# A decayed linear attention followed by two matrix products: four stages share a 512-column first product, and the whole program is written as one list

## The chip, the cores and the metric

The kernel runs on one core of a Trainium2 chip. A core has TensorE (PE, with its weight loads shown as PEld), VectorE (DVE), ScalarE (ACT), GpSimd (POOL) and SyncE (SP). Each engine executes its own instructions in the order in which the program lists them, and waits on semaphores for what other engines produce. The metric is the device time of one execution in microseconds (us), the median of several runs; lower is better.

## The reference

The first part is a recurrence over 768 tokens, for 4 batches and 8 heads of width 48. The second part is a two-layer product over all 3072 tokens.

```python
for t in range(S):
    cur = einsum('bhd,bhe->bhde', u * kt, vt)
    y[:, :, t] = einsum('bhd,bhde->bhe', rt, state + cur)
    state = w[:, :, None] * state + einsum('bhd,bhe->bhde', kt, vt)
x = y.transpose(0, 2, 1, 3).reshape(3072, 384)
h = x @ w_in                      # 384 -> 2048
out = maximum(0.01 * h, h) @ w_out   # 2048 -> 384
```

## The kernel before, in words

The tokens are cut into 24 stages of 128 tokens. Stage n is batch n mod 4 and block n div 4 of that batch, so the state that stage n produces is needed by stage n + 4. Operands are bf16, sums are float32. PSUM has 8 banks of 128 x 512 float32; a bank is taken by a product and given back when another engine has read it out, in the order of the list. Each operation of a stage has a letter, which the list ORDER uses with the stage's number:

- `r`, `k`, `v`: load of the stage's r, k, v block, issued on POOL (line 220; stage 0's r and k go over SP and ACT, line 211). `wi`, `wo`: a quarter of w_in, w_out, issued on POOL (lines 230, 234).
- `Pq`, `Pk`: r and k times a decay table, on DVE (line 361), into `qk`. `X..T`: transposing DMA of `qk` into `tp`, issued on SP (line 366), from stage 6 on. Stages 0 to 5 are transposed on PE instead (`T`, line 424) and copied out by ACT or DVE (`t`).
- `A`: the 128 x 128 score products of 8 heads on PE (line 453), into two banks. `Ma`, `Mb`: on DVE, the strictly causal part of each bank is written into `at` (line 466; line 462 for stages 0 to 3).
- `q`: the diagonal u term, three instructions on DVE (lines 390, 392, 394: `ku`, `rku`, and their sum per head `s_tok`). `Q`: two instructions on POOL (line 401) that write the diagonal matrices into `at`, ahead of `M`. For stages 0 to 3 the diagonal goes another way (`X`, `D`, and `Q` on DVE).
- `Y`: y of the stage, transposed, on PE (line 592): 12 products from the state and 16 from `at`, in strips of 32 columns. `y`: ACT copies it to `xT` (line 606).
- `K`: k-transposed times v on PE (line 494). `S`: the new state on DVE (lines 557, or 560 and 562).
- `G`, `J`: first product with w_in on PE, for one stage (128 columns, line 631) or a pair (256 columns, line 654); `g`, `j`: ACT applies the leaky relu and writes `gT` (lines 641, 664). `H`: second product with w_out on PE, 16 matmuls of 384 columns (line 678); `h`: ACT copies it out (line 690) and SP stores it (line 692).
- `F`: n matmuls on a tile of ones whose result is not used (line 267). `E`, `TQ`, `TK`, `Cw`, `Cu`, `C`, `W`, `U` and their like prepare tables.

The program is written by ORDER up to the first products of the pair 2 (stages 4 and 5) and the loads of stage 11. Then a loop takes pair m = 3 to 11: 8 first products `J` with their `j`; among or behind them `A` of the next pair; `P`, `X` of the pair after it, `M`, the loads three pairs ahead (held back until a product of the pair has been done), `q` and `Q`; `H` of the pair m - 1, with `Y`, `K`, `S` of the next pair between its two halves. The last `H` is split in two so that its store is short. `Sched.add` notes for each operation what it reads and writes, and `resolve` turns these into semaphore waits: one engine's order is the list's order, and a wait at the head of an engine holds everything behind it.

Of the kernel before, what the change touches and what calls it, by code (L numbers as in the profile page):

```python
# [30 lines left out]
T3q U t5q@ r4 t3q G2.1 Q1 utab A3 wi0 X3 g2.1 G0.3 M1b wo0 M3b D3 K3 g0.3 Y1 v5 M3a G2.3 y1 Q3 k6 G1.3 P4k g2.3 q5 k7
Y3 g1.3 T4k y3 v4 G1.1 t4k S3 G3.2 wo1 g1.1 P4q P5k G3.1 Q5 g3.2 S1 T5k g3.1 T4q G3.3 q4 t4q G0.0 t5k r6 g3.3 A4 A5
g0.0 P0k G3.0 Q4 M5a K0 G1.2 g3.0 M5b S0 K5 G2.2 g1.2 wo3 G2.0 M4a g2.2 wo2 P7k G1.0 g2.0 P6k M4b r7 K4 Y5 g1.0 S4 Y4
r9 y5 G0.2 S5 y4 k9 J2.7 g0.2 q6 r8 J2.5 j2.7 J2.6 k8 j2.5 J2.4 P6q j2.6 Q6 J2.0 X6T j2.4 J2.1 j2.0 J2.2 j2.1 k10 H2
j2.2 P7q q7 v6 X7T v7 P9q v8 H3 P9k h2 q9 X9T Q7 P8q H1 h3 Q9 q8 v9 P8k A6 h1 X8T A7 M6b H0 Q8 M6a M7b M7a v11 K7 Y6 h0
# [91 lines left out]
def bass_rwkv5_eagle__then__act_leaky_relu_kernel(  # L127
# [494 lines left out]
    def g1(n, grp):  # L622
        ps_g, key = g_bank[n, grp] = take()
        m, half = divmod(n, 2)
        ix, t = m % NX, slice(128 * half, 128 * half + 128)

        def emit():
            for f in range(4):
                fb = 4 * grp + f
                for s in range(NSL):  # L630
                    last = PE.matmul(ps_g[:, 128 * f:128 * f + 128], w_in_sb[:, s, 128 * fb:128 * fb + 128],  # L631
                                     xT[ix][:, s, t], start=s == 0, stop=s == NSL - 1)
# [12 lines left out]

    def g1_pair(m, j):
        ps_g, key = g_bank[m, j, 2] = take()
        ix = m % NX

        def emit():  # L650
            for f in range(2):
                fb = 2 * j + f
                for s in range(NSL):
# [176 lines left out]
```

## Time and profile before

| | |
|---|---|
| runs, median (lowest to highest) | 169.99 us (169.92 to 170.53), 3 runs |
| profiled execution | 170.09 us, span of its trace 168.3 us |
| granted TensorE clock, mean | 0.999 |
| PE busy | 161.6 us, 96% of the span |
| DVE, ACT, POOL busy | 110.2, 91.0, 111.1 us |
| data moved by DMA | 20.18 MB, mean 120 GB/s |

The profile gives, for each engine, groups of instructions with their busy time and the mean duration of one, the idle time ahead of them with what ended it, and the chain of work that ended last. A matmul's duration includes its way through the array and overlaps the next one's, so a product's cost is read from the distance between starts, not from its mean. A line of the timeline is: start, length, engine, line of the kernel, operation, output and inputs, shape, count, and in brackets the idle time before it and what ended that.

### The profile page before, as it was taken

What the parts mean: (1) busy time and instruction counts of PE and PEld (TensorE: products, weight loads), DVE (VectorE), ACT (ScalarE), POOL (GpSimd) and SP (SyncE); (2) the same over time, 40 slices, a digit from 0 to 9 for tenths busy, and PEclk for the clock granted to TensorE, in tenths of its full rate; (3) what the DMA queues carried; (4) which work ended last, traced back from release to release, by engine and by line L of the source; (5) the groups of instructions that cost most, each with busy time, mean ns of one, the idle gap of its engine ahead of it and who ended that gap; (6) DMA issues with size and microseconds to landing.
All of it is one profiled execution on the core that took longest, in us unless ns stands there. A gap on an engine that the chain in (4) does not pass through costs nothing.

```text
span 168.3 us, 4915 instructions
## 1 busy us (share of the span) xinstructions
PE 161.6 (96%) x2116; PEld 122.6 (73%) x2116; DVE 110.2 (66%) x221; ACT 91.0 (54%) x168; POOL 111.1 (66%) x125
## 2 busy tenths in 40 slices
PE   5889979999999999999999999999999999999994
PEld 5767869986568768768668768768678678668663
DVE  7499978828992497497599998996996805000000
ACT  4658777892228537537436536537537447449221
POOL 7999996999699929939939976975960540000000
PEclk9999999999999999999999999999999999999999
DMA  7999999999999996995994995994999111011012
GB/s 108 105 157 162 171 192 167 150 170 155 150 230 150 118 95 186 80 126 156 90 147 129 125 162 142 153 97 113 146 104 143 32 47 51 0 51 47 29 65 95
DMA packets 101263, 20.18 MB, mean 120 GB/s; under 512 B 94457, under 2 KB 101242, under 8 KB 101242
## 3 DMA queue, kind: packets, MB, share of 16 engines
q0 software_dynamic: 76512, 10.03, 93.3%
q1 hardware_dynamic: 23690, 9.64, 28.1%
q8 instruction: 16, 0.26, 0.7%
q10 hardware_dynamic: 1040, 0.20, 0.6%
q14 instruction: 5, 0.04, 0.1%
HBM read 20.45 MB, written 4.72 MB: 150 GB/s over the span
## 4 chain that ended last, share of the span: by engine, by line
PE 69%; POOL 12%; DMA 9%; DVE 7%; issue 1%; ACT 0%; POOLq 0%; DVEq 0%
PE ps L678 31%; PE ps L654 29%; DMA k_sb<-in_k_dram 5%; PE ps L592 5%; DMA r_sb<-in_r_dram 4%; POOL r_sb L220 3%; DVE qk L361 3%; PE ps L453 3%; POOL k_sb L220 3%; POOL v_sb L220 2%; PE ps L494 2%; DVE at L466 1%; POOL at L401 1%; POOL w_in_sb L230 1%; DVE rku L392 1%; DVE ku L390 1%
## 5 line engine op out<-in xcount | busy, mean ns | idle before, releaser
L678 PE MATMUL ps<-w_out_sb,gT 128*128 128x384 bf16 (+2 forms) x400 | 65.6, 320 | 0.0
L401 POOL TENSOR_TENSOR at<-ident,s_tok 128x512 bf16<-128x512 bf16 x40 | 42.8, 1101 | 21.0 <-DVE s_tok L394 21.0
L654 PE MATMUL ps<-xT,w_in_sb 128*128 128x256 bf16 x480 | 54.9, 273 | 0.0
L678 PEld LDWEIGHTS ps<-w_out_sb,gT 128*128 128x128 bf16 x400 | 37.7, 98 | 22.4
L664 ACT ACTIVATE gT<-ps 128x512 bf16<-128x512 f32 x80 | 47.8, 597 | 8.7 <-PE ps L654 4.0
L654 PEld LDWEIGHTS ps<-xT,w_in_sb 128*128 128x128 bf16 x480 | 46.4, 98 | 6.7
L690 ACT ACTIVATE out_sb<-ps 128x384 f32<-128x384 f32 (+2 forms) x25 | 12.0, 479 | 55.8 <-PE ps L678 55.8
L466 DVE CAST_PREDICATED at<-mask,ps 128x512 bf16<-128x512 uint16 x40 | 25.0, 684 | 21.8 <-PE ps L453 21.8
L220 POOL DMA_DIRECT2D k_sb<-in_k_dram x23 | 21.1, 923 | 3.3 <-PE ps L654 3.3
L220 POOL DMA_DIRECT2D v_sb<-in_v_dram x24 | 22.2, 925 | 0.8 <-POOLq L815 0.8
L220 POOL DMA_DIRECT2D r_sb<-in_r_dram x23 | 21.0, 914 | 0.0
L392 DVE TENSOR_TENSOR rku<-r_sb,ku 128x384 bf16<-128x384 bf16 x20 | 17.8, 892 | 0.7
L631 PE MATMUL ps<-xT,w_in_sb 128*128 128x128 bf16 x192 | 12.6, 219 | 0.5 <-DMA w_in_sb<-in_moe_w_in_dram 0.5
L606 ACT ACTIVATE xT<-ps 128x384 bf16<-128x384 f32 x24 | 10.9, 491 | 2.3 <-PE ps L592 2.2
L361 DVE TENSOR_TENSOR qk<-r_sb,qtab 128x384 bf16<-128x384 bf16 x23 | 9.1, 400 | 4.5 <-DMA r_sb<-in_r_dram 4.1
L631 PEld LDWEIGHTS ps<-xT,w_in_sb 128*128 128x128 bf16 x192 | 10.9, 98 | 1.3 <-DMA w_in_sb<-in_moe_w_in_dram 0.7
L394 DVE TENSOR_REDUCE s_tok<-rku 128x8 f32<-128x384 bf16 x20 | 11.1, 553 | 0.7
L641 ACT ACTIVATE gT<-ps 128x512 bf16<-128x512 f32 x16 | 9.5, 599 | 3.4 <-PE ps L631 2.9
L562 DVE TENSOR_TENSOR st<-sum_t,wl 128x384 bf16<-128x384 bf16 x16 | 10.7, 672 | 0.5
L592 PE MATMUL ps<-at,v_sb 128*32 128x128 bf16 x384 | 10.7, 219 | 0.0
L361 DVE TENSOR_TENSOR qk<-k_sb,ktab 128x384 bf16<-128x384 bf16 x23 | 9.9, 434 | 0.7 <-DMA k_sb<-in_k_dram 0.7
L592 PEld LDWEIGHTS ps<-tp,st 128*32 128x32 bf16 x240 | 7.2, 96 | 3.1 <-issue 2.5
(64 smaller groups left out, 120.9 us busy)
## 6 DMA issues: line engine op xcount, KB each, us to landing
out_dram<-out_sb SPq DMA_DIRECT2D x23, 192.0 KB, 2.2
v_sb<-in_v_dram POOLq DMA_DIRECT2D x24, 96.0 KB, 5.3
r_sb<-in_r_dram POOLq DMA_DIRECT2D x23, 96.0 KB, 5.4
k_sb<-in_k_dram POOLq DMA_DIRECT2D x23, 96.0 KB, 5.1
w_in_sb<-in_moe_w_in_dram POOLq DMA_DIRECT2D x4, 384.0 KB, 7.0
w_out_sb<-in_moe_w_out_dram POOLq DMA_DIRECT2D x4, 384.0 KB, 8.5
tp<-qk SPq DMA_TRANSPOSE x18, 4.1
k_f<-in_k_dram ACTq DMA_DIRECT2D x1, 192.0 KB, 2.8
```

The source lines that it names most:

```text
L220: add("pool", lambda: G.dma_start(dst, src), R=pace, W=[(which, n)], dma=f"{which}{n}")
L361: add("dve", lambda: V.tensor_tensor(qk[iq][:, H * half:H * half + H, 0:D], hd(src), hd(tab[:, :]), ALU.mult), R=[(name, n), "qk"[half] + ...
L392: add("dve", lambda: V.tensor_tensor(rku[i2][:, :], r_of(n), ku[i2][:, :], ALU.mult), R=[("r", n), ("ku", i2)], W=[("rku", i2)])
L394: add("dve", lambda: V.tensor_reduce(s_tok[i2][:, :], hd(rku[i2][:, :]), AX.X, ALU.add), R=[("rku", i2)], W=[("s", i2)])
L401: add("pool", lambda hh=hh, s_of=s_of: G.tensor_tensor(at[ia][:, hh, :, :], ident[:, :].unsqueeze(1).to_broadcast([128, NP, 128]), s_of.un ...
L466: add("dve", lambda: V.copy_predicated(at[n % NAT][:, hh, :, :], mask[:, :].bitcast(mybir.dt.uint16).unsqueeze(1).to_broadcast([128, NP, 1 ...
L592: last = PE.matmul(ps_y[32 * q:32 * q + 32, 128 * s:128 * s + 128], a, m, start=not whole and step == 0, stop=step == len(columns[q]) - 1)
L631: last = PE.matmul(ps_g[:, 128 * f:128 * f + 128], w_in_sb[:, s, 128 * fb:128 * fb + 128], xT[ix][:, s, t], start=s == 0, stop=s == NSL - 1)
L654: last = PE.matmul(ps_g[:, 256 * f:256 * f + 256], w_in_sb[:, s, 128 * fb:128 * fb + 128], xT[ix][:, s, :], start=s == 0, stop=s == NSL - 1)
L664: add("act", lambda: A.activation(gT[ig][:, 2 * j:2 * j + 2, :].rearrange("p f t -> p (f t)"), ps_g[:, :], AF.Prelu, alpha=0.01), R=[key], ...
L678: last = PE.matmul(ps_o[:, 0:c1 - c0], gT[ig][:, s, 128 * half:128 * half + 128], w_out_sb[:, s, c0:c1], start=s == 0, stop=s == NFB - 1)
L690: add("act", lambda: A.activation(out_sb[io][:, c0:c1], ps_o[:, 0:c1 - c0], AF.Copy), R=[key], W=held)
```

## The change

From stage 8 on four stages share a first product: `Z` takes one 128-column block of w_in against the 512 token columns of four stages (3 matmuls of 512 columns, filling one bank), and `z` reads the bank out. `xT` and `gT` become two buffers of 512 columns in place of three of 256. Stages 0 to 3 keep `G`, stages 4 to 7 keep `J`. `Y` of the four stages of a group stands in one run on PE; some `A` stand right behind a `Y` run. The loop is gone: one ORDER lists all operations on all engines, the early ones too, in a new order. The loads are no longer held back by products; on POOL they stand where the list has them. `F` is 16 matmuls in all, in place of 55. The number of all other operations is the same.

```diff
-FIRST, NB, PACE = 6, B, 3
-TURNED, DIAG, CARRY, EXACT, RAW, VISIT, LATE = 6, 4, 4, 1, 1, 3, 3
+NB = B
+TURNED, DIAG, CARRY, EXACT, RAW = 6, 4, 4, 1, 1
 ORDER = """
-w8 k0 r0 u8 u v0z v0 ones table v0y tcol trow r2 tri id wlz id8 k2 zr F18 Cw c0k Wl wi1 F4 T0k qk0 E r5 c0q F10 T0q wu8
...
-r10 S7 Y7 y6 K6 k11 y7 J2.3 S6 v10 j2.3 r11
+w8 qk0 k0 table c0k wi1 v0y tcol trow id id8 zr ones wlz Cw Wl E r1 k1 v0 r0 c0q F3 u8 T0k F13 wu8 v0z T0q Cu TQ u tri
+u16 t0k W t0q X0 qtab TK ktab A0 k2 P1q T1q k3 P1k C D0 M0b t1q M0a T1k t1k U utab A1 Q0 P2k Y0 X1 D1 P3k T2k r2 y0 P2q
+M1b t2k r3 P3q T3k M1a T2q v1 v2 G0.1 t2q T3q Q1 X2 wi0 t3k A2 t3q K1 M2b Y1 A3 v3 r5 r4 D2 K2 y1 M2a Q2 M3a G1.1 g1.1
+M3b k4 k5 Y2 y2 wi3 G0.0 X3 g0.0 G2.0 D3 S2 g0.1 wi2 P0k K3 G1.0 P4q Q3 g1.0 G2.1 P5q Y3 v4 v5 wo3 S1 wo0 y3 g2.1 T4q
+wo2 P4k T4k P5k T5q q5 t4k t4q G3.1 g3.1 wo1 Q5 q4 t5q@ Q4 r8 G3.0 g3.0 G1.3 g1.3 K0 T5k t5k S3 G3.3 A4 g3.3 A5 M5a
+G2.3 M5b M4a G2.2 G1.2 g2.3 g2.2 k7 G0.3 k6 Y5 r6 S0 M4b Y4 y5 k8 G3.2 y4 g3.2 G0.2 J2.2 J2.0 g0.3 r7 K5 j2.2 g0.2 k9
+r9 J2.5 S5 J2.4 g1.2 j2.5 J2.1 J2.7 j2.1 q6 j2.4 r10 q8 K4 P7k P7q X7T g2.0 r11 J2.6 j2.6 J2.3 k11 H3 P9k k10 H1 q7
+P11q P6q P6k X6T j2.7 P9q P11k H2 S4 v6 P8k H0 Q6 j2.3 j2.0 H5 Q8 h1 q10 P10q Q7 A7 X11T P10k P8q X10T X8T h3 h5 q11
+M7b A6 M6a M7a v7 Q10 H4 M6b Y7 h0 y7 q9 Y6 Q11 A11 y6 A10 M11b K7 S7 J3.5 M11a J3.4 j3.4 J3.3 j3.3 M10b M10a j3.5 X9T
+J3.0 j3.0 J3.1 j3.1 h2 J3.2 j3.2 K6 S6 v11 J3.6 Q9 A8 A9 h4 M8b J3.7 v8 K8 K11 Y11 M8a M9a M9b Y8 v10 Y10 j3.6 v9 S11
+r15 P15q j3.7 Y9 y9 r12 P12q y8 k15 y11 y10 H6 k13 Z2.9 Z2.2 Z2.13 z2.13 r13 k12 q15 q13 Z2.7 Z2.15 K10 z2.9 z2.15 v12
+k14 P12k X12T q12 z2.2 K9 P15k X15T Z2.4 v13 S10 z2.7 r14 P13q Z2.5 Z2.11 Z2.14 Z2.1 P14k P13k z2.11 z2.5 P14q Q15 z2.4
+X13T S9 Z2.3 Z2.10 X14T z2.14 Q13 h6 z2.3 Q12 v15 r17 z2.10 q14 Z2.0 A12 A15 v14 Q14 H7 M12b k21 M12a M15b r21 r18 h7
+S8 M15a k18 Z2.12 v18 A13 M13a z2.1 A14 M13b z2.0 M14a Z2.8 K12 M14b Z2.6 z2.12 z2.6 S12 z2.8 Y13 y13 Y12 Y15 q18 Y14
+r16 H10 y14 P17q y15 k17 y12 K14 Z3.15 h10 k16 K15 P18q S15 P18k Z3.8 X18T z3.8 r19 P16q r22 Z3.11 z3.11 Z3.7 z3.7 v19
+K13 S13 Z3.9 Z3.3 Z3.1 q17 q16 P16k z3.3 X16T P19q Z3.6 Z3.0 z3.9 z3.0 Z3.2 z3.2 S14 Z3.14 Z3.4 H11 z3.4 z3.14 P21k
+z3.1 Z3.12 k19 z3.12 P19k X19T A18 r20 Z3.5 z3.15 k20 P17k X17T Q17 q21 P20q Q18 q19 z3.5 Z3.10 P20k X20T M18b h11 Q16
+z3.10 v17 H8 v16 M18a Q19 P22q z3.6 q20 A16 P21q X21T Q20 v22 A17 A19 M17a H9 M19b M16b h9 K19 Y18 y18 M19a v23 M16a
+Y16 y16 M17b Y17 y17 Y19 y19 A20 k22 M20a A21 h8 S19 Q21 K18 Z3.13 z3.13 Z4.9 z4.9 K17 M21b S17 Z4.8 Z4.13 r23 z4.13
+M20b Z4.5 z4.5 Z4.6 z4.8 Z4.11 K16 P22k Z4.7 X22T q22 S16 H12 Z4.2 z4.2 k23 P23k P23q H14 H13 z4.11 z4.7 X23T z4.6 h14
+A22 q23 Q23 v21 A23 M21a v20 M23a h13 H15 M23b h15 Y21 y21 Y20 y20 Y23 y23 Q22 M22a M22b S18 Y22 Z4.3 y22 Z5.14 Z5.1
+z5.1 Z5.6 Z5.11 h12 z4.3 Z4.10 Z5.5 Z5.13 z4.10 Z5.2 z5.2 z5.13 Z4.4 z4.4 z5.5 Z5.0 z5.0 Z5.10 z5.11 Z5.12 Z4.0 z5.12
+Z5.9 z5.9 z5.14 Z4.14 Z4.12 Z4.1 z4.1 z4.0 Z5.7 Z4.15 Z5.4 z4.15 z5.10 z4.12 z4.14 Z5.8 z5.8 Z5.3 z5.7 Z5.15 z5.15 z5.3
+H16 H19 H18 h19 h18 h16 H17 z5.6 z5.4 H22 H20 h22 h20 h17 H21 h21
 """
...
-    NQK, NTP, NVS, NAT, NT, NX, NG, NO = 6, 6, 6, 6, 10, 3, 3, 4
+    NQK, NTP, NVS, NAT, NT, NX, NG, NO = 6, 6, 6, 6, 10, 2, 2, 4
...
-    xT = [SB(f"xT{i}", [128, NSL, 256]) for i in range(NX)]
-    gT = [SB(f"gT{i}", [128, NFB, 256]) for i in range(NG)]
+    xT = [SB(f"xT{i}", [128, NSL, 512]) for i in range(NX)]
+    gT = [SB(f"gT{i}", [128, NFB, 512]) for i in range(NG)]
...
+    def g1_wide(n0, width, fb0, count):
+        ps_g, key = g_bank[n0, width, fb0] = take()
+        ix, slots = n0 // 4 % NX, range(n0 % 4, n0 % 4 + width)
+        t, step = slice(128 * slots[0], 128 * slots[0] + 128 * width), 128 * width
+
+        def emit():
+            for f in range(count):
+                fb = fb0 + f
                 for s in range(NSL):
+                    last = PE.matmul(ps_g[:, step * f:step * f + step], w_in_sb[:, s, 128 * fb:128 * fb + 128],
                                      xT[ix][:, s, t], start=s == 0, stop=s == NSL - 1)
             return last
 
+        add("pe", emit, R=[("xT", ix, slot) for slot in slots] + [("win", fb0 // 4)],
+            W=[key] + [("pace", n0 + i, fb0) for i in range(width)])
+
+    def g1_wide_out(n0, width, fb0, count):
+        ps_g, key = g_bank[n0, width, fb0]
+        ig, slots = n0 // 4 % NG, range(n0 % 4, n0 % 4 + width)
+        t = slice(128 * slots[0], 128 * slots[0] + 128 * width)
+        add("act", lambda: A.activation(gT[ig][:, fb0:fb0 + count, t],
+                                        ps_g[:, :].rearrange("p (f t) -> p f t", t=128 * width), AF.Prelu, alpha=0.01),
+            R=[key], W=[("gT", ig, slot, fb0 + f) for slot in slots for f in range(count)])
         give(key)
 
...
+        "G": lambda n, x: g1_wide(n, 1, 4 * int(x[1:]), 4), "g": lambda n, x: g1_wide_out(n, 1, 4 * int(x[1:]), 4),
+        "J": lambda n, x: g1_wide(2 * n, 2, 2 * int(x[1:]), 2), "j": lambda n, x: g1_wide_out(2 * n, 2, 2 * int(x[1:]), 2),
+        "Z": lambda n, x: g1_wide(4 * n, 4, int(x[1:]), 1), "z": lambda n, x: g1_wide_out(4 * n, 4, int(x[1:]), 1),
...
-        "L": lambda n, x: load_stage(n, pace=[("pace", PACE, 0)]),
+        "L": lambda n, x: load_stage(n),
...
-    for m in range(FIRST // 2, NST // 2):
...
+    run(ORDER)
```

More of the change, by code (lines that the diff above doesn't have):

```diff
@@ L31 @@
[L31 to L35, printed above, removed]
@@ L646, in g1_pair @@
[L646 to L653, printed above, removed]
-                    last = PE.matmul(ps_g[:, 256 * f:256 * f + 256], w_in_sb[:, s, 128 * fb:128 * fb + 128],
-                                     xT[ix][:, s, :], start=s == 0, stop=s == NSL - 1)
-            return last
-        add("pe", emit, R=[("xT", ix, 0), ("xT", ix, 1), ("win", j // 2)],
-            W=[key, ("pace", 2 * m, j), ("pace", 2 * m + 1, j)])
```

88 lines of the change are left out of this document (13 added, 75 removed).

## The prediction

> **What bounds the kernel now.** I read the page's busy times first, then the chain that ended last, then the timelines of PE, DVE and POOL, then the landing times of the DMAs.
>
> ```profile
> PE 161.6 (96%) x2116; PEld 122.6 (73%) x2116; DVE 110.2 (66%) x221; ACT 91.0 (54%) x168; POOL 111.1 (66%) x125
> PE 69%; POOL 12%; DMA 9%; DVE 7%; issue 1%; ACT 0%; POOLq 0%; DVEq 0%
> ```
>
> The chain in order of time (start, length, what) says where PE takes over:
>
> ```profile
> 15.61 7.52 DMA r_sb<-in_r_dram
> ...
> 32.27 8.17 DMA k_sb<-in_k_dram
> ...
> 49.90 0.57 PE ps L592 x28
> ...
> 57.20 2.71 PE ps L678 x16
> 59.91 0.90 PE ps L592 x56
> 60.80 0.45 PE ps L494 x8
> 61.25 2.60 PE ps L678 x16
> 63.85 5.24 PE ps L654 x48
> ...
> 88.73 1.97 PE ps L654 x18
> 90.70 0.55 PE ps L453 x16
> 91.25 3.38 PE ps L654 x30
> ...
> 155.50 10.45 PE ps L678 x80
> 165.95 0.02 issue
> ```
>
> From 49.90 to 165.95 the chain is PE alone, back to back: in the loop nothing waits. Before that loads, DVE and POOL set the pace. So the change can win PE time everywhere, but it gives up the loop, in which DVE and POOL ran well ahead of PE. The question is whether they can still keep up with a list in which a whole group of four must be ready at once.
>
> **PE's own work.** The chain gives prices: 256 columns 5.24 / 48 = 109.2 ns, 384 columns 2.60 / 16 = 162.5 ns; the line through both gives 55.9 ns for 128 and 215.8 ns for 512. One `Z` costs 0.65 us, the 16 of a group 10.36 us against 10.48 us for two pairs: 0.12 us a group, 0.5 us in all. That is all that 512 columns give. A `Y` run of one stage takes 0.57 us, of two 0.90 us, so 0.33 us a stage and 0.24 us for entering; a run of four is then 1.56 us against 1.80 us, 1.0 us in four groups. An `A` pair is 0.55 us; behind it H takes 2.71 instead of 2.60 us, and `J` split by it 1.97 + 3.38 = 5.35 instead of 5.24 us: about 0.1 us for each change of shape. The new list has 9 runs of `A`, the loop split its `J` besides, which saves some 0.6 us.
>
> The Trainium skill, "TensorEngine Tiling (Array Packing)", Key Properties, says that changing the tiling mode drains the engine; the 0.1 and 0.24 us above are what the trace shows of it.
>
> Common checkpoint: all first products of stages 0 to 5 done (G and J2).
>
> ```profile
> 22.99 1.51 PE L631 MATMUL ps<-xT,w_in_sb 128*128 128x128 bf16 x24 [0.51 <-DMA w_in_sb<-in_moe_w_in_dram]
> 25.00 0.62 PE L424 MATMUL ps<-ident,qk 128*128 128x128 bf16 x8 [0.50 <-DVE qk L361]
> 32.99 4.75 PE L654 MATMUL ps<-xT,w_in_sb 128*128 128x256 bf16 x42
> 37.57 7.96 PE L678 MATMUL ps<-w_out_sb,gT 128*128 128x384 bf16 x48
> ```
>
> Before stands at 37.57 us with 42 of the 48 matmuls of J2 behind it, so at 38.2 us with the last six (0.66 us). It then needs 127.7 us. The new list needs behind the checkpoint: H 62.45 (23 x 2.60 + 2.65), J3 5.24, Z 41.4, A 4.95 and 0.9 for its runs, Y 0.90 + 4 x 1.56 = 7.1, K 14 x 0.23 = 3.2: 125.3 us if PE never waits. **First term: -2.4 us** (bounds -3.0 and -1.8: with and without the 0.1 us entries).
>
> **The start.** The list is led by DVE there. Durations for following it, DVE first, then POOL:
>
> ```profile
> 57.09 2.48 DVE L466 CAST_PREDICATED at<-mask,ps 128x512 bf16<-128x512 uint16 x4 [5.35 <-PE ps L453]
> 59.49 0.35 DVE L361 TENSOR_TENSOR qk<-r_sb,qtab 128x384 bf16<-128x384 bf16 x1
> 59.76 0.35 DVE L361 TENSOR_TENSOR qk<-k_sb,ktab 128x384 bf16<-128x384 bf16 x1
> ...
> 60.56 0.35 DVE L390 TENSOR_TENSOR ku<-k_sb,u_tab 128x384 bf16<-128x384 bf16 x1
> 60.95 0.36 DVE L392 TENSOR_TENSOR rku<-r_sb,ku 128x384 bf16<-128x384 bf16 x1
> 61.34 0.55 DVE L394 TENSOR_REDUCE s_tok<-rku 128x8 f32<-128x384 bf16 x1
> 61.81 0.35 DVE L390 TENSOR_TENSOR ku<-k_sb,u_tab 128x384 bf16<-128x384 bf16 x1
> 62.20 1.08 DVE L392 TENSOR_TENSOR rku<-r_sb,ku 128x384 bf16<-128x384 bf16 x1
> ...
> 64.36 1.03 DVE L562 TENSOR_TENSOR st<-sum_t,wl 128x384 bf16<-128x384 bf16 x1
> ```
>
> ```profile
> 61.98 4.32 POOL L401 TENSOR_TENSOR at<-ident,s_tok 128x512 bf16<-128x512 bf16 x4 [3.07 <-DVE s_tok L394]
> ...
> 92.06 0.88 POOL L220 DMA_DIRECT2D r_sb<-in_r_dram  x1
> 92.93 0.90 POOL L220 DMA_DIRECT2D v_sb<-in_v_dram  x1
> ```
>
> From start to start: half a mask 0.60, half a `P` 0.27, a stage's `q` 1.25, a state 0.92 us on DVE; on POOL a load 0.87, a stage's `Q` 2.1 us. On POOL the new list issues stages 0 to 5 and all eight weights without a diagonal between, the last at 22 us. Landings, of r6 in the list before (two lines) and of the transposes (two lines):
>
> ```profile
> L220 POOL DMA_DIRECT2D r_sb<-in_r_dram x1: 970/970/970, 24.3 to 24.3; - x1
> DMA to landing us min/median/max: 8.0/8.0/8.0
> tp<-qk SPq DMA_TRANSPOSE x18, 4.1
> DMA to landing us min/median/max: 2.7/4.1/7.4
> ```
>
> r4 (issued at 15.61, 7.52 us to land) came at 23.1 and held DVE and, at 25.00, PE; now it is issued at 13.3 with one weight fewer ahead and lands at about 19. Following PE and DVE by these durations, Y0 ends at 12.0, Y1 at 15.2, Y3 at 20.9, Y4 at 29.4, and J2 at 36.4 us: masks, `P` and states of DVE set each of these `Y`, then PE's own G and J2 behind Y4 take the rest. **Second term: -1.8 us** (bounds -2.8, if no DVE wait is left, and +0.5, the third rival below).
>
> **What the groups of four wait for.** Followed without any wait, by the prices above, PE reaches A7 at 49.4 (36.4 + 5 x 2.60); Y6 ends at 53.7 (A 0.65, H4 2.60, Y 0.90), Y9 at 62.7 (J3 5.24, two pairs of A 1.3, K 0.7, Y 1.56), Y14 at 81.8 (two H, 16 Z, A, K, Y: 5.2 + 10.4 + 1.3 + 0.7 + 1.56), Y19 at 105.7 (four H, 15 Z and the same), Y22 at 125.4 (four H, 9 Z), and the last H at 161.8. What must be there by then comes from DVE and POOL, and they hinder each other. `rku` took 0.36 us at 60.95 with POOL idle and 1.08 us at 62.20 with a diagonal of 1.04 us running; `st` 1.03 us at 64.36. Over the run:
>
> ```profile
> L392 DVE TENSOR_TENSOR rku<-r_sb,ku 128x384 bf16<-128x384 bf16 x20 | 17.8, 892 | 0.7
> L562 DVE TENSOR_TENSOR st<-sum_t,wl 128x384 bf16<-128x384 bf16 x16 | 10.7, 672 | 0.5
> ```
>
> Against 360 ns undisturbed that is (892 - 360) x 20 + (672 - 360) x 16 = 15.6 us, with the `P` about 19 us, or 0.95 us for each of the 20 stages that have a `Q`. In the loop it cost nothing, because DVE's cover was the idle time that `M` spends waiting for PE. In the new list `P`, `q`, `S` and `M` stand packed around runs of `Q`, so I charge 1.0 us a stage (bounds 0, and 1.5 if both diagonals of a stage hold one instruction each).
>
> The Trainium skill, "SBUF — State Buffer", Who interferes with whom, has the rule: a VectorE instruction with two SBUF inputs and a GpSimd instruction that reads SBUF exclude each other for the whole instruction. The rows agree (0.36 against 1.08 us); by the rule alone each of a stage's two diagonals could hold one instruction, and the sum below would come, as an estimate, to about 175 us.
>
> - **Stages 6 and 7.** 16 loads and eight weights are queued ahead; r6, issued at 29.4, lands 8.0 us later, 37.4. DVE waits there, then does q6, q8, P7, P9k, q7, P11q, P6: 4.1 us and 3 x 1.0 for Q6, Q8, Q7, with r7 and r6 between them 45.9 us. X6T lands 4.1 (median) to 7.4 us later, I take 5.0, near the median: A6 at 50.9 instead of 49.7. Behind it M7, M6, q9, M11b, S7 hold J3.3 (its bank is freed by S7) to 57.8, and S6, M8, M9 and the load v9 (POOL, behind Q9) hold Y9 to 64.6. Late by 1.9 us.
> - **Stages 12 to 15.** Z2.14 waits for the bank of S10 (0.45 us), A13 and A14 for X13T and X14T, whose `P` stand behind q12, S10 and the diagonals of 15, 13, 12. Late by another 1.5 us.
> - **Stages 16 to 19.** POOL issues 14 loads in a row (12.2 us), then Q17, Q18, Q16. DVE has 13.4 us of work between M14b and M18b, a wait of about 3 us for k18 and 4 to 5 us of hindrance by the diagonals; A17 needs M18b's bank and X17T and has 18.8 us from Y14. Late by 1.7 us there and by 0.9 us at M16 and M17.
> - **Stages 20 to 23.** v20, almost last on POOL, lands as Y20 is due; H12, H14, H13, H15 give DVE room. Nothing.
>
> ACT keeps up with `Z` (0.60 us, the row below, against 0.65 us) and PSUM's eight banks cover its order. **Third term: +6.0 us** (bounds 0 and +9.6). What else the list moves costs nothing as long as PE is busy: stores on SP stand between transposes, but wait only for `H` that are done.
>
> ```profile
> L664 ACT ACTIVATE gT<-ps 128x512 bf16<-128x512 f32 x80 | 47.8, 597 | 8.7 <-PE ps L654 4.0
> ```
>
> **Sum.** The profiled execution took 170.09 us, 1.8 us more than its span and 0.1 us over the median of the runs. 170.09 - 2.4 - 1.8 + 6.0 = 171.9, as a median 171.8 us. The runs lie within 0.4%, so 0.5% (0.85 us) is about what can be told from no change.
>
> **The rivals.**
> - *DVE and POOL keep up* (faster). The place is M18b, X6T and S10; the price 1.04 us for each diagonal that meets a two-input instruction. Without that hindrance X6T lands at 49.0 against 49.4, and every later step meets PE within half a microsecond; below about 0.4 us a stage nothing waits beyond the 0.2 to 0.5 us that before shows at 49.90. For it: DVE and POOL are both idle a third of the span. Against it: the mean of 892 ns. The time is 170 - 4.2 + 1.5 = 167.3 us (165.8 to 169.1). Chance 0.34.
> - *It cancels.* Half of the waits, 3.5 to 5 us: 169.2 to 170.8 us. Chance 0.15.
> - *The start is not won.* The first POOL load is now wi1, 384 KB ahead of r1 and k1 and beside k0 and r0, and PE lacks the early fills. They ran at 2.10 / 18 = 117 ns each at first and at 66 ns later:
>
> ```profile
> 1.33 2.10 PE L267 MATMUL ps<-ones 128*128 128x128 bf16 x18 [1.33 <-DVE ones L257]
> 10.08 1.06 PE L267 MATMUL ps<-ones 128*128 128x128 bf16 x16
> ```
>
>   If PE stays slow for 3 us longer and k0 is 0.7 us late, the start is 0.5 us behind before instead of 1.8 us ahead: 174.1 us. Chance 0.10.
>
> The forecast has 0.41, with its own range 170.8 to 173.2. Faster 0.34, same 0.15, slower 0.51. The range reaches into the first rival to 166.8 and past the third to 175.0.
>
> **What would show it.** Right: J2 ends near 36.4 us, Z at 216 ns, PE idle for about 6 us between 49 and 112 us, ended by transposes, masks and states; rku's mean stays near 0.9 us; PE unbroken from the last Y on. Wrong: PE without waits behind 49 us, or an end of J2 behind 38 us.

## The result, and the profile after

The change makes the kernel slower: 181.39 us (180.29 to 184.06, 4 runs) against 169.95 us (169.66 to 170.53, 4 runs) for the kernel before on the same chip, a ratio of 1.065 (95% interval 1.055 to 1.075). The forecast was 171.8 us with a range up to 175.0. Medians below are of all executions of a kernel; ratios leave out those over 1.5% above its fastest, so that some rest on few (2 of 10 in e9, 2 of 4 in e8, 5 of 10 in v1, 7 of 9 in v6) and are lower than the quotient of the medians.

The page of the profiled execution (182.5 us, span 180.5 us): busy times, then shares of the chain that ended last by engine.

```profile
PE 163.9 (91%) x1885; PEld 104.5 (58%) x1885; DVE 108.8 (60%) x221; ACT 83.9 (46%) x168; POOL 110.8 (61%) x125
PE 59%; DVE 23%; DMA 7%; ACT 3%; POOL 3%; issue 3%; DVEq 0%; ACTq 0%
```

DVE has no more to do than before, yet its share of the chain went from 7 to 23%: PE now waits for it. Where, the windows view shows, cut at the ends of J2, Y9, Y14, Y19, Y22 and the last `H` (columns: busy time and count of each engine, clock, DMA share and rate):

```profile
39.50:68.20 28.70, 26.84 (x378) 18.23 (x376) 26.92 (x44) 9.58 (x20) 22.13 (x24) 1.00 1.12 129
68.20:93.00 24.80, 20.91 (x248) 10.82 (x236) 19.36 (x37) 11.47 (x23) 22.43 (x24) 0.93 1.57 127
93.00:122.00 29.00, 25.89 (x281) 14.33 (x275) 22.62 (x45) 12.09 (x24) 22.85 (x25) 0.94 1.31 122
122.00:141.70 19.70, 19.70 (x248) 11.68 (x245) 11.52 (x25) 8.40 (x18) 7.38 (x8) 1.00 0.62 86
141.70:178.30 36.60, 36.49 (x216) 20.29 (x216) 0.00 (x0) 16.98 (x36) 0.00 (x0) 1.00 0.12 44
```

PE is idle 1.9, 3.9 and 3.1 us in the first three stretches and 0.1 us behind 122 us. In the first DVE is busy 94% of the time, against 66% of before's whole span. The forecast gave the five stretches, following PE without a wait, 26.3, 19.1, 23.9, 19.7 and 36.4 us: they came late by 2.4, 5.7, 5.1, 0.0 and 0.2 us. Beside the 8.9 us of idle time, the clock column (0.93 and 0.94) takes 0.07 x 24.8 + 0.06 x 29.0 = 3.5 us. Some 0.3 us of that falls into idle time (0.7 us at half rate ahead of 79.31, below), so idle time and clock make up about 12 of the 13.2 us by which the first three stretches came late. PE's timeline names what it waited for (in brackets), with the slow start ahead:

```profile
13.93 1.49 PE L648 MATMUL ps<-xT,w_in_sb 128*128 128x128 bf16 x12
...
18.12 0.84 PE L648 MATMUL ps<-xT,w_in_sb 128*128 128x128 bf16 x12
...
39.53 1.79 PE L672 MATMUL ps<-w_out_sb,gT 128*128 128x384 bf16 x10
...
57.15 0.24 PE L609 MATMUL ps<-tp,st 128*32 128x128 bf16 x4 [0.70 <-issue]
61.90 2.14 PE L648 MATMUL ps<-xT,w_in_sb 128*128 128x256 bf16 x18 [0.84 <-DVE at L483]
79.31 4.75 PE L648 MATMUL ps<-xT,w_in_sb 128*128 128x512 bf16 x15 [2.74 <-DVE sum_t L577]
89.44 0.40 PE L470 MATMUL ps<-tp 48*128 48x128 bf16 x8 [1.15 <-ACT gT L659]
115.10 0.62 PE L470 MATMUL ps<-tp 48*128 48x128 bf16 x16 [3.11 <-DMA tp<-qk]
115.65 4.45 PE L672 MATMUL ps<-w_out_sb,gT 128*128 128x384 bf16 x16
```

J2 ends at 39.5 (the next line's start); 12 first products took 1.49 us at 13.93 and 0.84 at 18.12. At 79.31 Z2.14 waits 2.74 us for the bank that S10 reads, at 115.10 A17 waits 3.11 us for X17T. Behind both, PE is slow as well: 15 matmuls of 512 columns took 4.75 us (317 ns each), 16 of 384 columns 4.45 us instead of 2.60. The granted clock (the number after the engines) says why, in steps of 2 us:

```profile
76.00:78.00 2.00, 0.58 (x3) 0.08 (x1) 1.93 (x3) 1.39 (x3) 1.72 (x2) 1.00 0.58 131
78.00:80.00 2.00, 0.69 (x2) 0.28 (x3) 1.97 (x5) 0.19 (x1) 1.40 (x2) 0.66 0.00 0
80.00:82.00 2.00, 2.00 (x6) 0.73 (x5) 2.00 (x5) 0.98 (x2) 2.00 (x3) 0.50 0.58 131
82.00:84.00 2.00, 2.00 (x12) 0.70 (x9) 1.83 (x5) 1.15 (x2) 1.44 (x2) 0.99 1.29 109
```

The clock was at half rate for 2 x (0.34 + 0.50 + 0.01) / 0.5 = 3.4 us. DVE's `P` groups in before, the groups of DVE and POOL in after, and the two rows that show DVE held most plainly, DVE first, then POOL:

```profile
L361 DVE TENSOR_TENSOR qk<-k_sb,ktab 128x384 bf16<-128x384 bf16 x23 | 9.9, 434 | 0.7 <-DMA k_sb<-in_k_dram 0.7
L361 DVE TENSOR_TENSOR qk<-r_sb,qtab 128x384 bf16<-128x384 bf16 x23 | 9.1, 400 | 4.5 <-DMA r_sb<-in_r_dram 4.1 <-ACT qtab L320 0.4
```

```profile
L378 DVE TENSOR_TENSOR qk<-k_sb,ktab 128x384 bf16<-128x384 bf16 x23 | 14.9, 661 | 1.8 <-PE ps L511 1.7
L378 DVE TENSOR_TENSOR qk<-r_sb,qtab 128x384 bf16<-128x384 bf16 x23 | 12.8, 563 | 2.9 <-DMA r_sb<-in_r_dram 2.7
L409 DVE TENSOR_TENSOR rku<-r_sb,ku 128x384 bf16<-128x384 bf16 x20 | 10.8, 540 | 0.7
L579 DVE TENSOR_TENSOR st<-sum_t,wl 128x384 bf16<-128x384 bf16 x16 | 7.1, 446 | 0.6
L418 POOL TENSOR_TENSOR at<-ident,s_tok 128x512 bf16<-128x512 bf16 x40 | 42.6, 1095 | 26.1 <-DVE s_tok L411 26.0
```

```profile
39.72 3.60 DVE L378 TENSOR_TENSOR qk<-k_sb,ktab 128x384 bf16<-128x384 bf16 x1
39.97 4.25 POOL L418 TENSOR_TENSOR at<-ident,s_tok 128x512 bf16<-128x512 bf16 x4
```

P7k, 0.35 us of work, took 3.60 us beside four diagonals back to back.

### The profile page after: what moved, and what is told of

It is laid out like the page before. It is cut to its first block, busy times and chain, and to the rows that moved or that the text cites. A ratio compares the mean times of both kernels' runs of the same rounds, so it can differ in the third digit from the quotient of the medians.

```text
span 180.5 us, 4459 instructions
## 1 busy us (share of the span) xinstructions
PE 163.9 (91%) x1885; PEld 104.5 (58%) x1885; DVE 108.8 (60%) x221; ACT 83.9 (46%) x168; POOL 110.8 (61%) x125
## 4 chain that ended last, share of the span: by engine, by line
PE 59%; DVE 23%; DMA 7%; ACT 3%; POOL 3%; issue 3%; DVEq 0%; ACTq 0%
PE ps L648 24%; PE ps L672 23%; DVE qk L378 9%; PE ps L609 4%; DVE rku L409 4%; DMA r_sb<-in_r_dram 4%; DVE s_tok L411 3%; DMA tp<-qk 3%; PE ps L470 3%; DVE ku L407 2%; PE ps L441 2%; PE ps L511 1%; POOL v_sb L237 1%; DVE sum_t L577 1%; DVE at L483 1%
## 5 line engine op out<-in xcount | busy, mean ns | idle before, releaser
L648 PE MATMUL ps<-xT,w_in_sb 128*128 128x128 bf16 (+2 forms) x480 | 69.9, 300 | 4.6 <-DVE sum_t L577 2.7
L659 ACT ACTIVATE gT<-ps 128x512 bf16<-128x512 f32 x96 | 52.4, 603 | 33.7 <-PE ps L648 33.2
L418 POOL TENSOR_TENSOR at<-ident,s_tok 128x512 bf16<-128x512 bf16 x40 | 42.6, 1095 | 26.1 <-DVE s_tok L411 26.0
L648 PEld LDWEIGHTS ps<-xT,w_in_sb 128*128 128x128 bf16 x480 | 38.7, 100 | 27.8 <-DVE sum_t L577 3.2
L483 DVE CAST_PREDICATED at<-mask,ps 128x512 bf16<-128x512 uint16 x40 | 25.4, 684 | 10.3 <-PE ps L470 10.2
L378 DVE TENSOR_TENSOR qk<-k_sb,ktab 128x384 bf16<-128x384 bf16 x23 | 14.9, 661 | 1.8 <-PE ps L511 1.7
L577 DVE TENSOR_TENSOR sum_t<-ps,st 128x384 bf16<-128x384 f32 x16 | 8.8, 551 | 8.7 <-PE ps L511 8.7
L470 PE MATMUL ps<-tp 48*128 48x128 bf16 x192 | 9.0, 228 | 4.9 <-DMA tp<-qk 3.4
L409 DVE TENSOR_TENSOR rku<-r_sb,ku 128x384 bf16<-128x384 bf16 x20 | 10.8, 540 | 0.7
L470 PEld LDWEIGHTS ps<-tp 48*128 48x128 bf16 x192 | 5.9, 98 | 9.1 <-issue 6.4
L609 PE MATMUL ps<-tp,st 128*32 128x128 bf16 x240 | 8.9, 220 | 0.7 <-issue 0.7
L609 PEld LDWEIGHTS ps<-at,v_sb 128*32 128x32 bf16 x384 | 8.8, 98 | 0.6 <-issue 0.4
```

The source lines that it names most:

```text
L378: add("dve", lambda: V.tensor_tensor(qk[iq][:, H * half:H * half + H, 0:D], hd(src), hd(tab[:, :]), ALU.mult), R=[(name, n), "qk"[half] + ...
L409: add("dve", lambda: V.tensor_tensor(rku[i2][:, :], r_of(n), ku[i2][:, :], ALU.mult), R=[("r", n), ("ku", i2)], W=[("rku", i2)])
L418: add("pool", lambda hh=hh, s_of=s_of: G.tensor_tensor(at[ia][:, hh, :, :], ident[:, :].unsqueeze(1).to_broadcast([128, NP, 128]), s_of.un ...
L470: last = PE.matmul(at_bank[n][hh][0][:, 128 * p:128 * p + 128], tp[it][rows, NP + p, :], tp[it][rows, p, :], start=True, stop=True)
L483: add("dve", lambda: V.copy_predicated(at[n % NAT][:, hh, :, :], mask[:, :].bitcast(mybir.dt.uint16).unsqueeze(1).to_broadcast([128, NP, 1 ...
L609: last = PE.matmul(ps_y[32 * q:32 * q + 32, 128 * s:128 * s + 128], a, m, start=not whole and step == 0, stop=step == len(columns[q]) - 1)
```

## The experiments

The theory: POOL's diagonals hold DVE's two-input instructions, and since DVE's work for four stages now stands right ahead of what PE waits for, the holding reaches PE. The rivals: a slow start, late loads, POOL's own time, the 512 columns, the half clock.

**e3: the holding and POOL's time away.** POOL writes the same tiles with an iota that reads nothing. The diagonal of stages 4 to 23 is left out of the result, in e5, e6, e8 and e11 too.

```diff
-            add("pool", lambda hh=hh, s_of=s_of: G.tensor_tensor(
-                at[ia][:, hh, :, :], ident[:, :].unsqueeze(1).to_broadcast([128, NP, 128]),
-                s_of.unsqueeze(2).to_broadcast([128, NP, 128]), ALU.mult),
+            add("pool", lambda hh=hh: G.iota(at[ia][:, hh, :, :], pattern=[[0, NP], [0, 128]], base=0, channel_multiplier=0,
+                                             allow_small_or_imprecise_dtypes=True),
                 R=["ident", ("s", n % 4)], W=[("at", ia, hh)])
```

> The changed kernel with the diagonal matrices left out: POOL fills these tiles with zeros by an instruction that reads nothing from SBUF (its length is not known beforehand, some 0.5 to 1 us against 1.04), with the same waits and the same readers. So POOL is busy in the same places, but no longer reads beside DVE. Theory 'hindrance' (VectorE instructions with two SBUF inputs wait for POOL's reads): rku, P and st fall from means of 540, 563 to 661 and above to 0.36 us, DVE gains some 12 to 19 us in all, the waits at J3.3, Z2.14 and A17 shrink from 0.8, 2.7 and 3.1 us to under 1 us each, the clock stays up, and the total falls by 6 to 10 us, to 171 to 175 us. Rival 'loads': DVE waits for r12 at 71.5 us and for k18 at 93 us as before, the waits of PE shrink by less than half, and the total falls by less than 4 us.

168.37 us (167.82 to 168.95), ratio 0.990 (0.986 to 0.994): 13.0 us less than after. Groups of e3, the windows line from just behind J2's end (37.65 by the cut used above) to PE's last, and the chain's shares:

```profile
L417 POOL IOTA at<- 128x512 bf16 x40 | 22.0, 579 | 30.4 <-DVE s_tok L411 30.3
L378 DVE TENSOR_TENSOR qk<-r_sb,qtab 128x384 bf16<-128x384 bf16 x23 | 7.8, 352 | 0.2 <-ACT qtab L337 0.2
L378 DVE TENSOR_TENSOR qk<-k_sb,ktab 128x384 bf16<-128x384 bf16 x23 | 7.8, 353 | 1.7 <-PE ps L509 1.7
L409 DVE TENSOR_TENSOR rku<-r_sb,ku 128x384 bf16<-128x384 bf16 x20 | 7.2, 358 | 1.3 <-DMA r_sb<-in_r_dram 0.7
L577 DVE TENSOR_TENSOR st<-sum_t,wl 128x384 bf16<-128x384 bf16 x16 | 5.7, 358 | 0.6
```

```profile
37.80:163.40 125.60, 125.57 (x1345) 74.36 (x1342) 65.92 (x155) 57.65 (x117) 55.29 (x77) 1.00 1.02 110
```

```profile
PE 93%; DVE 3%; ACT 2%; issue 1%; ACTq 0%
```

PE runs 125.6 us without a gap at full clock. Against e3's 352, 353, 358 and 358 ns, after's `P`, `rku` and `st` cost 4.9 + 7.1 + 3.6 + 1.4 = 17.0 us more, 0.85 us for each stage with a `Q`.

**e6: POOL's time given back, the holding not.** Two iotas in place of each diagonal.

```diff
+            for twice in range(2):
+                add("pool", lambda hh=hh: G.iota(
+                    at[ia][:, hh, :, :], pattern=[[0, NP], [0, 128]], base=0, channel_multiplier=0,
+                    allow_small_or_imprecise_dtypes=True),
+                    R=["ident", ("s", n % 4)] + [("at", ia, hh)] * twice, W=[("at", ia, hh)])
```

> The kernel after, with two iotas of zeros one behind the other in place of each diagonal product (the diagonal is left out): POOL is busy as long as in after (twice 579 ns for 1095 ns), but reads no SBUF. It splits what e3 changed at once. Theory (the holding of DVE is what costs): 168.0 to 170.0, with rku and P at their undisturbed 350 to 360 ns. Rival (POOL's time is what costs: diagonals that are ready late, loads issued late behind them): 175 or more, near the 181.4 of after.

170.24 us (169.24 to 171.46), ratio 1.002 (1.000 to 1.004).

```profile
L418 POOL IOTA at<- 128x512 bf16 x80 | 44.8, 578 | 12.4 <-DVE s_tok L411 8.8
```

POOL is as busy as in after and the time stays 11.2 us below it. By the medians, 1.9 of e3's 13.0 us were POOL's time and the rest the holding.

**e5: the same on the kernel before**, with e3's edit.

> The kernel before, with POOL's diagonals replaced by an iota of zeros as in e3 (the diagonal of stages 4 to 23 is left out of the result). It tells whether the loop of before paid for the same holding of DVE by POOL. Theory (POOL's reads hold DVE; in before this lay beside PE's work, since behind J2 its PE runs 127.7 us almost without a wait): 169.0 to 170.5, with rku at 358 ns instead of a mean of 892, and PE's last work no earlier than before by more than 1 us. Rival (before pays for it too, so that taking it away is worth the same 13 us in any order): under 165, and then what e3 won says nothing about the change.

169.46 us (168.61 to 170.65), ratio 0.998 (0.995 to 1.001), rku 358 ns throughout. Before had more of this holding in its rku (892 ns) and paid no more for it than the 0.6 us between the medians, which lies within the spread: there it lay beside PE's work.

**e9: a diagonal that reads less,** with the whole result.

```diff
+            add("pool", lambda hh=hh, s_of=s_of: G.affine_select(
+                at[ia][:, hh, :, :], s_of.unsqueeze(2).to_broadcast([128, NP, 128]),
+                [[0, NP], [-1, 128]], ALU.is_equal, 0.0, base=0, channel_multiplier=1),
+                R=[("s", n % 4)], W=[("at", ia, hh)])
```

> The kernel after, with each diagonal product on POOL (two operands of 512 columns read, 1095 ns) replaced by an affine select that reads only the row sums and writes them where column equals row, 0 elsewhere: the whole result is computed. Its duration is taken as near the iota's 579 ns (the nearest row), so POOL's time is about e3's. Theory (a POOL instruction that reads SBUF holds DVE's two-input operations for its length): the holding is halved, so the time lies between e3's 168.4 and after's 181.4, near 172 to 176, with rku at 400 to 600 ns. Rival (POOL's time alone counts): the same as e3, 168 to 169. Rival (a select costs more than the product, over 1.2 us): slower than after.

173.75 us (170.39 to 175.26), by the medians 2.2% over before; ratio 1.006 (1.003 to 1.010).

```profile
L418 POOL TENSOR_SCALAR_AFFINE_SELECT at<-s_tok 128x512 bf16<-128x512 f32 x40 | 26.0, 681 | 32.6 <-DVE s_tok L411 32.6
L409 DVE TENSOR_TENSOR rku<-r_sb,ku 128x384 bf16<-128x384 bf16 x20 | 9.2, 459 | 1.1 <-DMA r_sb<-in_r_dram 0.4
```

A select on POOL is 0.1 us longer than the iota and 0.4 us shorter than the product, and it still holds DVE, though less (rku 459 ns, against 358 and 540): the time lies between e3 and after, as the theory had it.

**e1 and e2: the slow PE.** e1 lists 18 fills first; e2 keeps PE busy with 40 and 44 fills ahead of Z2.14 and A17.

```diff
-w8 qk0 k0 table c0k wi1 v0y tcol trow id id8 zr ones wlz Cw
+w8 ones F18 qk0 k0 table c0k wi1 v0y tcol trow id id8 zr wlz Cw
```

```diff
-Z2.5 Z2.11 Z2.14 Z2.1
+Z2.5 Z2.11 f40.1 Z2.14 Z2.1
...
-Q20 v22 A17 A19
+Q20 v22 f44.2 A17 A19
```

> The changed kernel with 18 unused matmuls at the head of PE's list and the tile of ones written first on DVE, as the kernel before has them. In the changed kernel PE's matmuls of 128 columns stay near 110 to 125 ns apart until about 17 us (12 first products in 1.49 us at 13.9 us; before, 0.83 us), and the first products of stages 0 to 5 end at 39.5 us instead of the forecast 36.4. Theory 'cold start': PE is slow there because it did nothing until 3.7 us; with the 18 matmuls the first G takes 0.83 us again, the checkpoint comes 1.5 to 2.5 us earlier (37 to 38 us), and the total falls by 0.5 to 2.5 us, less where DVE and loads hold the later stages anyway. Rival 'the order itself': matmuls get fast at the same moment or the checkpoint stays within 0.4 us of 39.5; total unchanged.

> The changed kernel with 40 unused matmuls of 128 columns (2.2 us) ahead of Z2.14 and 44 (2.5 us) ahead of A17, on banks that are free; these are the two places where PE waited 2.74 and 3.11 us and where the granted clock then stood at 0.50 for 3.4 us each. Theory 'clock': with PE busy through the waits the granted clock stays at 1.0, 15 Z behind the first wait take 3.2 instead of 4.75 us and the 16 matmuls of H9 2.6 instead of 4.4 us, and the total falls by 2.5 to 3.4 us (to about 178 us). Rival 'the waits alone': the clock does not follow the waits, or what is won is waited for at the next place; the total falls by less than 0.8 us.

e1: 182.93 us (182.40 to 184.32). J2 ended at 38.4 instead of 39.5, the 12 first products at 14.14 still took 1.49 us, and nothing of it reached the end. (e7 below has no such fills and J2 at 38.4 too, so that the fills won the 1.1 us isn't shown.) e2: 180.90 us (179.41 to 182.43); the mean clock rose from 0.981 to 0.991, but Y22 ended at 141.67 as in after (141.69). Both half-rate stretches were gone, and a new one (90.88 to 94.30) stood behind a wait of 2.13 us at 89.48. What PE lost at half rate in these two places is time that it would have waited anyway.

**e4: 256 columns in place of 512.**

```diff
+            if width == 4:
+                for c in (0, 256):
+                    for s in range(NSL):
+                        last = PE.matmul(ps_g[:, c:c + 256], w_in_sb[:, s, 128 * fb0:128 * fb0 + 128],
+                                         xT[ix][:, s, c:c + 256], start=s == 0, stop=s == NSL - 1)
+                return last
```

> The changed kernel with each Z (3 matmuls of 512 columns) made of 6 matmuls of 256 columns into the same bank, everything else alike. By the first term of the forecast a Z then takes 0.655 instead of 0.647 us: 0.5 us over 64 of them, of which only the part in stretches where PE does not wait shows, so the total rises by 0 to 0.6 us, within the spread of the runs. Rival '512 columns matter' (in either direction): the total moves by more than 1.5 us, or the 72 matmuls of the last stretch, 15.66 us, become 144 in a time that differs from 15.7 by more than 0.5 us.

182.38 us (181.48 to 182.85). Five `Z` of e4, then of after:

```profile
124.25 3.44 PE L648 MATMUL ps<-xT,w_in_sb 128*128 128x256 bf16 x30
```

```profile
124.08 3.40 PE L648 MATMUL ps<-xT,w_in_sb 128*128 128x512 bf16 x15
```

0.04 us for five, 0.13 us for a group of 16 (the last 24 took 15.90 against 15.73 us): the 512 columns themselves are worth half a microsecond in all, as forecast. The median rose by 1.0 us, which after's spread (180.29 to 184.06) can't tell from that.

**e7: late loads.** r15, r12 and k15 earlier on POOL, into time that it waited.

```diff
-S4 v6 P8k H0 Q6 j2.3 j2.0 H5 Q8 h1
+S4 v6 r15 r12 P8k H0 Q6 j2.3 j2.0 H5 Q8 k15 h1
```

> The kernel after, with POOL's loads r15 and r12 issued right behind v6 and k15 right behind the diagonals of stage 8, in stretches where POOL waits for sums (2.41 and 1.61 us idle): they are issued some 12 us earlier, and the loads behind them some 2.7 us earlier. In after, DVE waited 2.72 us for r12. Theory (that wait is one delay in a chain that DVE's holding sets elsewhere too): the 2.72 us wait goes, the end moves by 0.5 to 2.7 us, to between 178.7 and 181. Rival (late loads are the main loss: r12, then k18 and the transposing DMAs behind them): 176 or less. No change at all, 181 to 182, would say that the wait hid something else of the same length.

181.11 us (179.91 to 182.77): nothing that the spread lets be told. DVE's 2.72 us wait for r12 and PE's for S10 are gone, and others stand in their place:

```profile
53.97 0.40 PE L470 MATMUL ps<-tp 48*128 48x128 bf16 x8 [2.06 <-DMA tp<-qk]
...
81.65 0.40 PE L470 MATMUL ps<-tp 48*128 48x128 bf16 x8 [0.88 <-DMA tp<-qk]
86.92 0.40 PE L470 MATMUL ps<-tp 48*128 48x128 bf16 x8 [1.19 <-ACT gT L659]
```

**e8, v1, v4, v6 and e12: the start, and what can be mended.** e8 is e3 with `F18` first and `F16` ahead of A1; v1 is e9 with these fills and e7's loads; v4 has more fills; v6 is v4 with k6 and r6 earlier on POOL; e12 is v6's order with the change's own product. The lists of PE's first operations (after, v1, v4), then of POOL's around k6 (v4, v6):

```diff
-Cw F3 T0k F13 T0q Cu TQ TK A0 T1q D0 T1k U A1
+F18 Cw F3 T0k F13 T0q Cu TQ TK A0 T1q D0 T1k U F16 A1
+F25 Cw F3 T0k F16 T0q Cu TQ TK A0 F4 T1q F3 D0 T1k U F16 A1
```

```diff
-wo1 Q5 Q4 r8 k7 k6 r6 k8 r7 k9
+wo1 k6 r6 Q5 Q4 r8 k8 k7 r7 k9
```

> e3 (the diagonal left out, POOL's iotas in its place) with 18 fills listed first and 16 more ahead of A1. In e3 nothing behind the end of the second products' start waits, so what the start wins shows whole in the time; in after and e3 the matmuls of the start went at the slow rate (12 first products in 1.49 us) where before's went in 0.83 us. Theory (the start is late because PE is slow there, for want of fills): the 12 first products of G0.1 take 0.84 us, J2 ends at 36.4 to 37.2 instead of 37.81, and the time is 167.0 to 167.9 instead of 168.4. Rival (the start is set by DVE and transfers, and the 16 fills only take PE's time): J2 ends at 37.8 or later, time 168.3 to 169.5.

> The change with what the runs so far suggest put on it: the affine select of e9 for the diagonals, the earlier loads of e7 and the fills of e8. The whole result is computed. Theory (three causes that add: holding halved, late loads gone, a start at full rate): 169.0 to 171.0, at or just above before. Rival (the waits that are left sit one behind the other beneath the same DVE chain, so that only the select counts, as e7 won nothing): 171.5 to 174, as e9.

> v1 with PE's idle places of the first 10 us closed by fills: 25 instead of 18 ahead of the first product (0.77 us idle there in v1), 16 instead of 13 ahead of T0q (0.24 us), 4 ahead of T1q (0.31 us), 3 ahead of D0 (0.25 us). The whole result is computed. v1 and e8 each fell into two groups of times (167.6 and 169.4 to 170.7; 167.0 to 167.3 and 169.6 to 169.7), and the profiled ones, of the shorter kind, had PE at full rate from 8.3 us on and J2 done at 36.6. Theory (the longer kind are executions in which PE stays slow in the start): all times near 167 to 168.3, before less 1 to 1.7%. Rival (the two kinds come from somewhere else, the loop's waits): the median stays near 170.

> v4 with the loads k6 and r6 ahead of the diagonals of stages 5 and 4 on POOL (they stand behind those diagonals, r8 and k7 in v4), and then r8 k8 k7 r7. In v4 the start is won (J2 done at 35.9, first forecast 36.4) and the time is before's all the same: DVE waited 4.03 us for k6, until 36.98, with nothing else to do, and is what the loop waits for up to 78 us. The whole result is computed. Theory (behind the start DVE is the bound, and its first work waits for k6, so a start that is won on PE alone is handed back): k6 lands about 3 to 5 us earlier and the time is 166.5 to 168.3. Rival (the loop's own waits decide, whenever DVE begins): 169.3 to 170.5.

> v6's order with the change's own diagonals (the product on POOL): all that fills and the places of loads can mend, with the holding left as it is. The whole result is computed. Theory (of the change's loss of 11.4 us, most is the holding): 175 to 179. Rival (the late loads and the slow start are the larger part): 172 or less. If nothing is won, 180 to 182, the waits lie one behind another beneath DVE's held work.

| | median, lowest to highest (us) | quotient of the medians | ratio to before |
|---|---|---|---|
| e8 | 168.48, 167.01 to 169.73 | 0.991 | 0.983 (0.979 to 0.987) |
| v1 | 170.13, 167.57 to 170.67 | 1.001 | 0.997 (0.993 to 1.000) |
| v4 | 170.01, 169.50 to 170.89 | 1.000 | 1.001 (0.999 to 1.003) |
| v6 | 169.11, 167.18 to 170.59 | 0.995 | 0.990 (0.987 to 0.994) |
| e12 | 179.41, 178.06 to 179.85 | 1.055 | 1.053 (1.049 to 1.057) |

PE and DVE of v4:

```profile
13.06 0.83 PE L648 MATMUL ps<-xT,w_in_sb 128*128 128x128 bf16 x12
...
35.90 4.39 PE L672 MATMUL ps<-w_out_sb,gT 128*128 128x384 bf16 x26
```

```profile
36.98 0.36 DVE L407 TENSOR_TENSOR ku<-k_sb,u_tab 128x384 bf16<-128x384 bf16 x1 [4.03 <-DMA k_sb<-in_k_dram]
```

With PE at full rate J2 ends at 35.9 us, and v4 is no faster than before: DVE, the bound of what follows, does nothing until k6 lands. In v6 POOL issued k6 at 21.89, 5 us earlier, but the load then took 14.1 us, the longest of all, issued behind w_out's four quarters (issue, then the spread of the k loads):

```profile
21.89 1.01 POOL L238 DMA_DIRECT2D k_sb<-in_k_dram  x1
```

```profile
DMA to landing us min/median/max: 3.7/5.6/14.1
```

So DVE began 1.0 us earlier (35.98) and the time fell by 0.9 us, short of the theory's 166.5 to 168.3. v6 computes the whole result and is the only such version clearly below before: by 0.5% in the median and 1.0% in the ratio. e12, v6's order with the product, says what the start and the loads are worth by themselves: 2.0 us of the change's loss of 11.4. From e12 to v6 only the select is new, and it is worth 10.3 us. That the longer times of v1 and e8 (169.4 to 170.7, against 167.0 to 167.6) come from the start isn't borne out: v4, with a start at full rate and fewer gaps on PE, sat at 169.5 to 170.9. What makes them stays open.

**v2, v3, e11 and v5: another order of fours.** v2 has before's start, and from stage 8 on for each group, in this order:

```diff
+Y12 y12 Y13 y13 Y14 y14 Y15 y15 H8 h8 K12 S12 K13 S13 H9 h9 K14 S14 K15 S15 H10 h10 H11 h11 P18q P18k X18T P19q P19k
+X19T q16 Q16 q17 Q17 (loads 20, 21) q18 Q18 q19 Q19 (loads 22, 23) Z3.0-3 A16 Z3.4-5 A17 M16a M16b M17a M17b
+Z3.6-8 A18 Z3.9-10 A19 M18a M18b M19a M19b P20q P20k X20T P21q P21k X21T Z3.11-15
```

v3 has the select in it, e11 the iota; v5 moves v2's loads and states, so that DVE would wait for neither.

> The 512-column first products and the Y of four in the order of before: before's start word for word up to its first pair behind it, then from stage 8 on, by groups of four, four Y, the second products of the group before among K and states, DVE's P and row sums there, and the 16 first products with the next group's A and masks in their midst. Diagonals as in after (the product on POOL). The whole result is computed. Theory (the change's own saving on PE is 2.4 us, and its loss is the order, which puts DVE's P and row sums, held by POOL, right ahead of what PE waits for): with the DVE work of four stages lying beside some 24 us of H and Z, the holding is covered, and the time is before's less 1.5 to 2.4 us: 167.6 to 168.6. Rival (stages in fours need the undisturbed DVE whatever the order): 171 or more, with rku's mean over 500 ns and PE waiting for masks.

> v2 with the affine select of e9 in place of the diagonal product on POOL. The whole result is computed. Theory (in v2 the holding is covered): within 0.5 us of v2. Rival (it is not): faster than v2 by what v2 lost, 1 to 5 us.

> v2 with the iota of zeros in place of the diagonals (left out of the result), to split what v2 lost (182.2): the holding of DVE, or its own order, which issues r10 to r15 late (DVE waited 14.3 us for them) and puts loads between the diagonals, which the masks then wait for. Theory (v2 failed as the change does, by the holding): 167.5 to 169.5. Rival (v2's order costs by itself): 173 or more; from v3's 174.1, with the select, 170 to 172 would be some of each.

> v2 with its own faults mended: all four diagonals of a group ahead of the loads of the next on POOL, r and k ahead of v, K and states right behind the four Y, so that DVE waits for neither. Diagonals by the product, whole result. Theory of the holding (about 0.9 us of DVE per stage, here beside H and Z): 168 to 171 if the order covers it, which would make the change's loss one of where DVE's work stands. Rival (groups of four with the product can't be covered): 174 or more.

v2 182.21 us (ratio 1.074, 1.069 to 1.078), v3 174.07 (1.024, 1.020 to 1.027), e11 172.52 (1.019, 1.014 to 1.024), v5 182.02 (1.072, 1.068 to 1.076). v2's own order costs some 2.5 us over before (e11, where DVE waited 8.8 us for r loads, against 4.1 in before). The product in place of the iota costs another 9.7 us (v2 less e11): the holding and POOL's time, not split here. The select takes back 8.1 us of it. v5 gained nothing, but its loads were late as well. DVE's `P` in v2, then in v5:

```profile
L378 DVE TENSOR_TENSOR qk<-r_sb,qtab 128x384 bf16<-128x384 bf16 x23 | 8.7, 380 | 14.7 <-DMA r_sb<-in_r_dram 14.3 <-ACT qtab L337 0.4
```

```profile
L378 DVE TENSOR_TENSOR qk<-k_sb,ktab 128x384 bf16<-128x384 bf16 x23 | 9.7, 427 | 11.1 <-DMA k_sb<-in_k_dram 11.1
L378 DVE TENSOR_TENSOR qk<-r_sb,qtab 128x384 bf16<-128x384 bf16 x23 | 8.6, 379 | 8.3 <-DMA r_sb<-in_r_dram 7.9 <-ACT qtab L337 0.4
```

So my guess for v2, that an order of fours can cover the product, is borne out by neither list: in v2's the product costs about 10 us, in the change's 13. With DVE waiting for loads in both v2 and v5, that no order can isn't shown.

## Why the prediction was wrong

- **PE's own work, -2.4 us: right.** 125.3 us behind the end of J2 were forecast; e3, which has no wait there, took 125.7 us (37.65 to 163.37). Of it the 512 columns are half a microsecond (e4).
- **The start, -1.8 us: wrong, it was +1.3.** J2 ended at 39.5 us, which the prediction itself had named a sign of being wrong (behind 38). The failed step is the one that followed "PE and DVE by these durations" to J2 at 36.4 us, with PE at full rate from the first first products on. In after it was slow up to about 17 us. With PE fast J2 came at 35.9 to 36.6 us (e8, v1, v4, v6), so the DVE part of the step held. My third rival had the mechanism (PE slow for longer) at a chance of 0.10 and 0.5 us behind instead of 1.3. Part of the miss is luck: in e7, whose list is the same up to there, J2 ended at 38.4. And a start that is won need not be a gain: v4's was handed back at k6, and e8's J2 was 1.5 us ahead of e3's (36.1 against 37.7) with a median no lower.
- **The waits, +6.0 us: the mechanism right, the size wrong.** They came to 13.0 us (138.7 from J2's end to PE's last, less 125.7), beyond the upper bound of 9.6. The charge of 1.0 us a stage was near: 0.85. What failed is the step that turned the charge into waits. Stages 6 and 7, up to Y9, came late by 2.4 us (forecast 1.9) and stages 20 to 23 by nothing, as forecast. Stages 12 to 15 were put at 1.5 us and cost 5.7, stages 16 to 19 at 2.6 and cost 5.1. There I let each hold delay DVE by about its mean, gave Z2.14 0.45 us of waiting for S10 where it was 2.74, and left out r12, which landed 7.0 us after its issue and held DVE for 2.72 us, and the clock, which stood at half for 3.4 us at each of the two long waits. k18 was not the cause: I had put DVE's wait for it at 3 us, and it was 0.9. These do not add one by one: e7 took r12's wait away, e2 the two half-rate stretches, and neither won what the spread lets be told; they stand beneath DVE's chain, and only shortening that (e3, e6, e9) moved the end by much. How the 13 us split among them isn't shown.
- **"DVE and POOL keep up", 167.3 us:** with the holding away this is what happens, 168.4 us (e3). The row that decided against it, 892 ns for rku, was the right one to read, and its 540 ns in after would have misled: much of the holding moved to `P`, from 434 and 400 ns to 661 and 563.
- **Of the Trainium skill** I used "SBUF — State Buffer", Who interferes with whom, for an estimate of about 175 us by holds of one instruction's length. That section leaves out a GpSimd instruction that only writes; e3 and e6 agree, their iotas held nothing (rku 358 ns). Where it has the loser blocked for the length of the other's instruction, a sentence that it writes of VectorE's two-port modes and that I took over, P7k's 3.60 us beside diagonals of 1.06 us each shows one blocked through several. The measurement decides, and the price has no bound of one diagonal.

## What to carry to other kernels

An instruction that is slowed by a neighbour costs nothing as long as its engine waits for the bound engine anyway; before work is packed into larger groups, add up the slowed time in the busiest stretch, not over the run, and look for the longest single hold. Take the cause away in one run (an instruction that writes the same tile and reads nothing) before the list is tuned: the order was worth 2 us here and the other diagonal 10. A start that was won on PE showed here only in part (0.9 us), and only once the load that DVE waited for came earlier too.
